# A spectral-mixing and attention stack with its stages woven together: one arena for all layers, work moved across the layer borders, and another share between two softmax paths

## The chip, the cores and the metric

The kernel runs on one core of one Trainium2 chip. The metric is the time of one execution on the device in microseconds (us). The core has five engines that run their own instruction streams in order: PE (matrix multiply; PEld are its weight loads), DVE (vector), ACT (scalar, activation functions), POOL and SP (here it only starts DMAs). Matmul results land in PSUM, which has 8 banks of 128 x 512 float32 in this program's tiling; everything else lives in SBUF.

## The reference, cut to what matters

```
x = A_x                                  # 1 x 2048 x 512, bfloat16
for _ in range(2):
    X = rfft2(layernorm(x)) * (w_r + 1j * w_i)
    x = x + irfft2(X)                                    # layer A, spectral
    n = layernorm(x)
    q = (n @ wq).reshape(32 heads, 2048, 16);  k = n @ wk;  v = n @ wv     # one k, v for all heads
    o = softmax(q k^T / 4) v                             # per head
    x = x + o.reshape(2048, 512) @ wo                    # layer B, attention
```

## The kernel before, in words

The 2048 rows of x lie in SBUF as `x_sb[128, r, t, 512]` with r and t from 0 to 3. Four rows r of one t belong together: the layer norm of a group t (`LayerNorm`, L87) takes statistics of its four slices as each is finished (`add`, L93: `bn_stats`, `bn_aggr` on DVE), then two small operations on POOL for 1/sqrt(var + eps) (L109, L110) and four scalings on DVE (L112) into `xn_sb`.

**Layer A** (`spectral_layer`, L149) works in three stages. Stage 1 goes over t: DVE makes sums and differences over r (L158 to L161), PE transposes them (L168), 16 matmuls against a Fourier table follow (L177), and ACT and DVE write the result to `Y`. Stage 2 goes over four groups j2: 48 matmuls of Y against the table `TAB` (L197 to L201), ACT copies the sums out (L203), and DVE multiplies them with the weights and combines them into `V` (L208 to L222). Stage 3 goes over t: 16 matmuls on V (L246), a copy by ACT and sums by DVE into `AT` (L251 to L253), and for each r five matmuls, one of them adding x (L256, L260); ACT writes x back (L262) and the layer norm's `add` follows. `TAB` is loaded with two of its six slots; POOL makes the negated slots and the repeated ones (L80 to L83).

**Layer B** (`attention_layer`, L270) begins when layer A is over. For four chunks qc of 512 rows, PE transposes xn (L129), and multiplies with the k weights twice, once for each of two zero-padded copies `wka` (L305); then come the four q projections of the first chunk (L289) and the v projection of all rows (L318). Only then does the loop start.

**The loop** (`AttnLoop`, L333) is written out by hand, and its engines keep this order (`manual_schedule`). It goes over 4 blocks qb of 512 query rows, 8 steps s of four heads each, here called stripes, so a layer has 32 stripes. Of the 16 chunks kc of 128 keys, 11 take the ACT path: two score matmuls into a double PSUM tile `sa`, one exponential on ACT over both into `e` (L463), and two steps later two matmuls with v into `acc`. The 5 chunks of `D_KC` take the DVE path: one score matmul into `sd`, DVE turns it into an int16 whose bits are a coarse power of two (`t0`, L467), two shifted copies by DVE (`tj`, L425) and one by POOL (L431) serve as further terms, and four matmuls with four scaled copies of v add them up. A stripe is 22 steps (`do_step`, L444), each with one ACT-path pair; in 20 of them there is a DVE-path unit as well. The two without are steps 10 and 21 of the stripe. They also carry the pieces: q projections of the next qb (L296, in s = 3 and 4), and the output projections of the last qb (`project`, L406, in s = 1 and 2), which add to x and, in the first attention layer, run the layer norm (L414, L100, L101, L112). `sa` and `sd` have two buffers each.

When a stripe's sums are complete, about eight steps into the next stripe, ACT copies `acc` to `den` (L374); SP moves the 4 rows of sums out (`dq`), DVE takes reciprocals six steps later (L381), SP sends them through DRAM and spreads them over the partitions (`rd`, `rb`), and ten steps later DVE normalises (`on_new` L397 for even s, `odd` L400 for odd s, which four DMAs then place into `on`). After the last step the loop runs on without new scores until all is drained (L510).

Both layers open and close their own SBUF and PSUM pools, and `full_kernel` (L516) runs A, B, A, B.

## Time and profile before

| | us |
|---|---|
| median of 5 runs (lowest, highest) | 1721.61 (1720.59, 1726.83) |
| the profiled execution, as timed | 1722.28 |
| its span, first to last instruction | 1720.5 |
| first attention loop, first exponential to last copy of sums | 709.18 |
| second attention loop, the same | 689.18 |

In the rows of the profile, times are us unless marked ns. A row of a group gives line, engine, operation, output and input tiles, count, then busy time, mean ns of one, idle time of the engine just ahead of it and what ended that. A row of a timeline gives start, length, engine, line, operation, and in brackets the idle time ahead and who released it. A row of the windows view gives, for a stretch of the span, its length, busy time and count of each engine, the TensorE clock granted (1.00 is full), and DMA. Busy times of overlapping instructions of one engine are not counted twice in sums over a stretch, but the mean length of one instruction includes the overlap with its neighbour.

### The profile page before, as it was taken

What the parts mean: (1) busy time and instruction counts of PE and PEld (TensorE: products, weight loads), DVE (VectorE), ACT (ScalarE), POOL (GpSimd) and SP (SyncE); (2) the same over time, 40 slices, a digit from 0 to 9 for tenths busy, and PEclk for the clock granted to TensorE, in tenths of its full rate; (3) what the DMA queues carried; (4) which work ended last, traced back from release to release, by engine and by line L of the source; (5) the groups of instructions that cost most, each with busy time, mean ns of one, the idle gap of its engine ahead of it and who ended that gap; (6) DMA issues with size and microseconds to landing.
All of it is one profiled execution on the core that took longest, in us unless ns stands there. A gap on an engine that the chain in (4) does not pass through costs nothing.

```text
span 1720.5 us, 34822 instructions
## 1 busy us (share of the span) xinstructions
PE 1535.9 (89%) x13536; PEld 484.5 (28%) x13536; DVE 1477.0 (86%) x2534; ACT 1427.0 (83%) x1607; POOL 720.8 (42%) x704
## 2 busy tenths in 40 slices
PE   0987999998999899989959799999999999999995
PEld 0543222222222222222225332222222222222221
DVE  3675999999999999999966769999999999999995
ACT  0434999998999899989923369999999999999993
POOL 6000444544444444444510115454545454545443
PEclk9998999999999999999989989999999999999997
DMA  6000000000000000000000000000000000000000
GB/s 175 1 1 1 8 16 16 16 16 16 16 16 16 11 15 17 15 15 16 16 15 1 1 1 15 16 16 16 28 16 16 16 28 16 16 16 28 16 16 29
DMA packets 39541, 31.78 MB, mean 18 GB/s; under 512 B 20800, under 2 KB 30160, under 8 KB 39248
## 3 DMA queue, kind: packets, MB, share of 16 engines
q1 hardware_dynamic: 38416, 27.31, 5.4%
q8 instruction: 106, 1.74, 0.4%
q0 software_dynamic: 960, 2.25, 0.4%
q14 instruction: 59, 0.48, 0.1%
HBM read 24.30 MB, written 2.62 MB: 16 GB/s over the span
## 4 chain that ended last, share of the span: by engine, by line
PE 55%; DVE 23%; ACT 12%; issue 4%; DMA 2%; POOL 2%; SPq 0%; ACTq 0%; DVEq 0%; POOLq 0%
PE acc_new L365 25%; PE sd L352 15%; ACT e L463 10%; DVE t L467 9%; PE sa L352 5%; DVE tj L425 3%; DVE on_new L397 2%; PE ps L412 2%; DVE odd L400 2%; PE ps L289 2%; DVE stats L100 2%; PE ps L197 2%; PE ps L177 1%; ACT den L374 1%; DVE xn_sb L112 1%
## 5 line engine op out<-in xcount | busy, mean ns | idle before, releaser
L463 ACT ACTIVATE e<-sa 128x1024 bf16<-128x1024 f32 x1408 | 1320.7, 1100 | 54.7 <-PE sa L352 51.8
L431 POOL TENSOR_SCALAR t<-tj 128x1024 int16<-128x1024 int16 x640 | 671.6, 1049 | 761.9 <-DVE tj L425 544.7
L467 DVE TENSOR_SCALAR t<-sd 128x512 int16<-128x512 f32 x1280 | 829.8, 678 | 66.6 <-PE sd L352 61.9
L352 PE MATMUL sa<-QT,KT 32*128 32x512 bf16 x2816 | 551.5, 384 | 12.3 <-ACT e L463 11.9
L365 PE MATMUL acc_new<-e,V 128*32 128x512 bf16 x2816 | 557.0, 392 | 1.0 <-ACT e L463 1.0
L352 PE MATMUL sd<-QT,KT 32*128 32x512 bf16 x1280 | 493.6, 386 | 59.9 <-DVE t L467 59.0
L425 DVE TENSOR_SCALAR tj<-t 128x2048 int16<-128x2048 int16 x640 | 438.0, 685 | 0.0
L365 PE MATMUL acc_new<-t,V 128*32 128x512 bf16 x2560 | 388.2, 387 | 1.0 <-POOL t L431 1.0
L365 PE MATMUL acc_new<-tj,V 128*32 128x512 bf16 x2560 | 386.9, 386 | 2.4 <-DVE tj L425 2.4
L352 PEld LDWEIGHTS <-KT 32*128 32x128 bf16 x4096 | 197.3, 91 | 675.6 <-issue 674.8
L365 PEld LDWEIGHTS <-V 128*32 128x32 bf16 x7936 | 159.0, 93 | 330.8 <-issue 330.3
L109 POOL TENSOR_TENSOR rstd<-mv,eps 128x4 f32<-128x4 f32 x16 | 3.7, 233 | 202.5 <-DVE mv L101 202.4
L170 ACT COPY xT<-ps 128x1024 bf16<-128x1024 bf16 x8 | 8.1, 1012 | 69.4 <-PE ps L168 69.4
L412 PE MATMUL ps<-wo_sb,on_new 128*128 128x512 bf16 x128 | 36.6, 419 | 25.7 <-DMA on_new<-odd 25.7
L100 DVE BATCH_NORM_STATS2 stats<-x_sb 128x6 f32<-128x512 bf16 x64 | 42.4, 678 | 12.4 <-ACT x_sb L262 8.3
L112 DVE TENSOR_SCALAR xn_sb<-x_sb,mv,rstd 128x512 bf16<-128x512 bf16 x64 | 22.0, 409 | 35.8 <-POOL rstd L110 35.8
L400 DVE TENSOR_TENSOR odd<-den,rb 128x512 bf16<-128x512 f32 x32 | 38.8, 1212 | 13.1 <-DMA rb<-rd 13.1
L203 ACT CAST Xs<-ps 128x512 bf16<-128x512 f32 x32 | 18.8, 586 | 36.8 <-PE ps L201 36.8
L197 PE MATMUL ps<-Y,tab_TAB 128*128 128x512 bf16 x128 | 48.5, 379 | 0.0
L168 PE MATMUL ps<-tab_ident,ec 128*128 128x128 bf16 x64 | 5.7, 241 | 46.5 <-DVE ec L159 43.8
L374 ACT COPY den<-acc_new 128x512 f32<-128x512 f32 x64 | 39.1, 611 | 8.1 <-PE acc_new L365 8.1
L414 DVE TENSOR_TENSOR x_sb<-ps,x_sb 128x512 bf16<-128x512 f32 x32 | 22.1, 690 | 24.5 <-PE ps L412 24.3
(81 smaller groups left out, 712.0 us busy)
## 6 DMA issues: line engine op xcount, KB each, us to landing
rb<-rd SPq DMA_DIRECT2D x64, 256.0 KB
x_sb<-in_A_x_dram SPq DMA_DIRECT2D x4, 512.0 KB
on_new<-odd SPq DMA_DIRECT2D x128, 16.0 KB
tab_TAB<-const_TAB SPq DMA_DIRECT2D x1, 1024.0 KB
wr_sb<-in_A_w_r_dram SPq DMA_DIRECT2D x4, 256.0 KB
wi_sb<-in_A_w_i_dram SPq DMA_DIRECT2D x4, 256.0 KB
dq<-den SPq DMA_DIRECT2D x64, 8.0 KB
rd<-dq SPq DMA_DIRECT2D x64, 8.0 KB
```

The source lines that it names most:

```text
L100: nc.vector.bn_stats(stats, self.x_sb[:, r, t, :])
L112: nc.vector.tensor_scalar(out=self.xn_sb[:, r, t, :], in0=self.x_sb[:, r, t, :], scalar1=mv[:, r, 0:1], scalar2=rstd[:, r:r + 1], op0=ALU. ...
L197: nc.tensor.matmul(ps, lhsT=TAB[:, t, j2, (COS + n) % 4, :], rhs=yt, start=(t == 0), stop=False, skip_group_check=True)
L352: self.nc.tensor.matmul(out, lhsT=self.KT[32 * i:32 * i + 32, half, kc * P:(kc + 1) * P], rhs=self.QT[32 * i:32 * i + 32, g, qb * 512:(qb ...
L365: self.nc.tensor.matmul(self.acc[key][32 * i:32 * i + 32, :], lhsT=self.V4[:, kc, j, :], rhs=e, start=first, stop=False, skip_group_check= ...
L374: nc.scalar.copy(out=den, in_=self.acc.pop(key))
L400: nc.vector.tensor_tensor(out=odd, in0=den, in1=rb, op=ALU.mult)
L412: nc.tensor.matmul(ps, lhsT=on[:, g, qt * P:(qt + 1) * P], rhs=self.wo_sb[:, g, :], start=(g == 0), stop=(g == 3))
L425: nc.vector.tensor_scalar(out=tj, in0=cyc["t0"], scalar1=float(SH[j]), scalar2=None, op0=ALU.add)
L431: nc.gpsimd.tensor_scalar(out=cyc["t1"][:, h, :], in0=tj[:, h, :], scalar1=1.0, scalar2=float(SH[1] - SH[j]), op0=ALU.mult, op1=ALU.add)
L463: nc.scalar.activation(out=e, in_=sa, func=ACT.Exp, bias=EXP_LN, scale=SCALE)
L467: nc.vector.tensor_scalar(out=self.dcyc[c]["t0"][:, k, :], in0=sd, scalar1=Y_MUL, scalar2=Y_ADD, op0=ALU.mult, op1=ALU.add)
```

## The change

The change rewrites how the layers are put together; what each engine computes for a layer is nearly the same.

- One SBUF arena and one PSUM arena serve the whole program (`Arena`, `make_arenas`). Tiles of layer A use the places of loop tiles (`ec` those of `t1`, `xTA` those of `t2`, `xc`, `dd`, `gh` those of `e`). PSUM is 2 double tiles "two", 2 tiles "one", 2 tiles "b", in banks as many as before. `den`, `rb` and `odd` have one buffer instead of two.
- At the start the first quarter of x is loaded first, then two small tables, then the other quarters, then the rest, all on SP. The layer norm and stage 1 of group t directly follow each other. The negated slots of TAB are made by ACT, the repeated ones by POOL, in the program's order after stage 1.
- The preparation of attention is cut by t (`prepare`): transposes, one k projection instead of two, whose two masked copies ACT and DVE write with `MASK`, and the v projection of that t. Each follows stage 3 of its t.
- ACT copies of stage 1 and 2 cover two banks where they covered one.
- In the loop, the normalisation is queued eight steps after the reciprocal and done just ahead of the next shift (`before_shift`). Pieces keep a distance of more than four steps. In the first attention layer, stripes s = 1 and 2 of qb = 1 to 3 have four DVE-path chunks and 24 steps, of which every third has no DVE-path unit. The last stripe of each loop has four DVE-path chunks, all in its first 16 steps. The four scalings of a layer norm are spread over four steps.
- What is left after the loop (`drain`) is outside the hand-written order, and so is stage 1 of the second layer A that follows.

```diff
+    nc.sync.dma_start(out=c.x_sb[:, :, 0, :], in_=x_v[:, :, 0, :])
+    table("ident")
+    table("PH")
+    for t in range(1, T):
+        nc.sync.dma_start(out=c.x_sb[:, :, t, :], in_=x_v[:, :, t, :])
...
+def expand_tab(nc, c):
     for u in range(4):
-        nc.gpsimd.tensor_scalar(out=tab[:, u, :, 2:4, :], in0=tab[:, u, :, 0:2, :], scalar1=-1.0, scalar2=None,
-                                op0=ALU.mult)
-        nc.gpsimd.tensor_copy(out=tab[:, u, :, 4:6, :], in_=tab[:, u, :, 0:2, :])
+        nc.scalar.mul(out=c.TAB[:, :, u, 2:4, :], in_=c.TAB[:, :, u, 0:2, :], mul=-1.0)
+        nc.gpsimd.tensor_copy(out=c.TAB[:, :, u, 4:6, :], in_=c.TAB[:, :, u, 0:2, :])
...
+    def prepare(self, t):
...
+        for cc in range(NC):
+            nc.tensor.matmul(pk, lhsT=c.wk[:, cc, :], rhs=xTq[:, cc, cols], start=(cc == 0), stop=(cc == NC - 1))
+        nc.scalar.activation(out=c.KT[:, 0, cols], in_=pk, func=ACT.Copy, scale=c.MASK[:, 0:1])
+        nc.vector.tensor_scalar(out=c.KT[:, 1, cols], in0=pk, scalar1=c.MASK[:, 1:2], scalar2=None, op0=ALU.mult)
...
+    def plan(self, qb, s):
+        if (qb, s) == (NQB - 1, 7):
+            return (1, 4, 7, 10), [a < 16 for a in range(24)]
+        if qb > 0 and s in (1, 2) and self.wide:
+            return (2, 5, 9, 12), [a % 3 != 2 for a in range(24)]
+        return (1, 4, 7, 10, 13), [a % 11 != 10 for a in range(22)]
...
-        self.at(10, lambda: self.normalize(key, den, rb))
+        self.at(8, lambda: self.before_shift.append(lambda: self.normalize(key, den, rb)))
...
     def shift(self, c, j):
         nc = self.nc
+        for fn in self.before_shift:
+            fn()
+        self.before_shift = []
...
-        if (d_unit is None or d_unit[0] is None) and self.pieces:
+        if u is None and self.pieces and self.step - self.last_piece > 4:
+            self.last_piece = self.step
             self.pieces.pop(0)()
...
+    for t in range(T):
+        for r in range(R):
+            ln_done(r, t)
+        spec.stage1(t)
+    expand_tab(nc, c)
+    for pair in range(n_pairs):
+        last = pair + 1 == n_pairs
+        spec.stage2()
+        at = Attention(nc, c, sb, ps, ln)
+        for t in range(T):
+            spec.final(t, ln_done)
+            if t == T - 1:
+                for g in range(4):
+                    at.qproj(0, g, g % 2 == 0)
+            at.prepare(t)
...
+        loop = AttnLoop(nc, c, at, work, dram, store if last else ln_loop, ln)
+        loop.wide = not last
+        with tc.manual_schedule(engines=LOOP_ENGINES):
+            loop.run()
+        loop.drain()
+        if not last:
+            spec = Spectral(nc, c, sb, ps, ln)
+            for t in range(T):
+                spec.stage1(t)
```

Three places show what this does to the order on an engine. On POOL at the start of the program, before, `rstd` is the layer norm's factor and `tab_TAB` the table:

```order
L109 TENSOR_TENSOR rstd<-mv,eps 128x4
L81 TENSOR_SCALAR tab_TAB<-tab_TAB 128x4x256
L83 COPY tab_TAB<-tab_TAB 128x4x256
L81 TENSOR_SCALAR tab_TAB<-tab_TAB 128x4x256
L83 COPY tab_TAB<-tab_TAB 128x4x256
L81 TENSOR_SCALAR tab_TAB<-tab_TAB 128x4x256
L83 COPY tab_TAB<-tab_TAB 128x4x256
L81 TENSOR_SCALAR tab_TAB<-tab_TAB 128x4x256
L83 COPY tab_TAB<-tab_TAB 128x4x256
L110 TENSOR_TENSOR rstd<-rstd,mhalf 128x4
```

The same place on POOL now:

```order
L169 TENSOR_TENSOR rstd<-mv,eps 128x4
L170 TENSOR_TENSOR rstd<-rstd,mhalf 128x4
L169 TENSOR_TENSOR rstd<-mv,eps 128x4
L170 TENSOR_TENSOR rstd<-rstd,mhalf 128x4
L144 COPY TAB<-TAB 128x4x256 x4
L169 TENSOR_TENSOR rstd<-mv,eps 128x4
```

The table's work stood between the two operations of the first layer norm; now the first two layer norms stand ahead of four copies, and the negations are gone from this engine.

On DVE at the end of the first attention loop, before, from the last shift; `odd` is the last normalisation, `x_sb` the output projection, `ec` and `xc` the inputs of stage 1:

```order
L425 TENSOR_SCALAR tj<-t_12485 128x2048
L381 RECIPROCAL dq<-dq 128x16
L400 TENSOR_TENSOR odd<-den,rb 128x512
L414 TENSOR_TENSOR x_sb<-ps,x_sb 128x512
L100 BN_STATS stats<-x_sb 128x6
L101 BN_AGGR mv<-stats 128x2
L414 TENSOR_TENSOR x_sb<-ps,x_sb 128x512
L100 BN_STATS stats<-x_sb 128x6
L101 BN_AGGR mv<-stats 128x2
L414 TENSOR_TENSOR x_sb<-ps,x_sb 128x512
L158 TENSOR_TENSOR ec<-xn_sb 128x1024
```

The same place on DVE now, from the third group's first sums:

```order
L200 TENSOR_TENSOR ec<-xn 128x1024
L201 TENSOR_TENSOR ec<-xn 128x1024
L418 RECIPROCAL dq<-dq 128x16
L202 TENSOR_TENSOR xc<-ec 128x512
L203 TENSOR_TENSOR xc<-ec 128x512
L225 TENSOR_TENSOR Y<-two,dd 128x256
L226 TENSOR_TENSOR Y<-two,dd 128x256
L227 TENSOR_TENSOR Y<-two,dd 128x256
L228 TENSOR_TENSOR Y<-two,dd 128x256
L213 COPY xTA<-one 128x1024
L434 TENSOR_TENSOR odd<-den,rb 128x512
```

Stage 1 of the groups whose layer norm is done stands around the last reciprocal and ahead of the last normalisation; before, it began after three of the four output projections.

On DVE in the loop, at the first normalisation (`on_new` before, `ON` now), in the second and third step of a stripe; `t` from `sd` or `b` is a score conversion, `t` or `tj` from `t` a shift. Before:

```order
L467 TENSOR_SCALAR t_1923<-sd 128x512 x2
L425 TENSOR_SCALAR tj<-t_1852 128x2048
L467 TENSOR_SCALAR t_1923<-sd 128x512
L397 TENSOR_TENSOR on_new<-den,rb 128x512
L467 TENSOR_SCALAR t_1923<-sd 128x512
```

Now:

```order
L492 TENSOR_SCALAR t_1872<-b 128x512 x2
L431 TENSOR_TENSOR ON<-den,rb 128x512
L459 TENSOR_SCALAR t_1897<-t_1801 128x2048
L492 TENSOR_SCALAR t_1872<-b 128x512 x2
```

The normalisation stands one conversion earlier, and the shift that stood ahead of it now stands behind it, so that both lie between the second and the third conversion of the stripe.

650 lines of the change are left out of this document (315 added, 335 removed), and 5 rows, old and new, of the table sb.

## The prediction

> **What bounds the kernel now.** I read the span stage by stage in the windows view, cut at the places where one stage hands over to the next. Its columns are the stretch, its length, the busy time of PE, PEld, DVE, ACT and POOL, the clock granted to TensorE, and DMA.
>
> ```profile
> 0.00:43.83 43.83, 0.00 (x0) 0.00 (x1) 17.64 (x53) 1.28 (x1) 29.93 (x32) 1.00 0.63 172
> 43.83:65.69 21.86, 20.84 (x128) 11.07 (x129) 14.02 (x33) 10.50 (x15) 0.00 (x0) 1.00 0.00 1
> 65.69:100.97 35.28, 32.44 (x213) 20.66 (x212) 26.25 (x51) 10.58 (x19) 0.00 (x0) 1.00 0.00 0
> 100.97:162.28 61.31, 49.28 (x306) 23.51 (x306) 36.24 (x81) 20.53 (x35) 4.83 (x8) 0.92 0.00 1
> 162.28:871.46 709.18, 663.93 (x6108) 185.82 (x6106) 654.08 (x1085) 671.61 (x735) 339.47 (x326) 0.99 0.05 15
> 871.46:914.40 42.94, 25.59 (x145) 12.71 (x145) 23.25 (x54) 11.09 (x16) 1.21 (x2) 0.80 0.03 8
> 914.40:949.50 35.10, 32.26 (x212) 20.58 (x211) 26.08 (x51) 10.60 (x19) 0.00 (x0) 1.00 0.01 1
> 949.50:1009.02 59.52, 47.59 (x306) 23.19 (x306) 36.23 (x81) 20.53 (x35) 4.83 (x8) 0.94 0.00 1
> 1009.02:1698.20 689.18, 658.20 (x6108) 185.11 (x6106) 639.51 (x1049) 669.74 (x736) 339.37 (x326) 1.00 0.06 18
> 1698.20:1720.50 22.30, 5.77 (x16) 1.80 (x15) 3.71 (x6) 0.57 (x1) 1.13 (x2) 0.58 0.12 39
> ```
>
> These ten add up to the span. The two attention loops are 1398 of 1720 us and full: ACT is busy for 95 and 97% of them. The other 322 us are not full: nothing runs on PE for 43.83 us at the start, and 100.97 to 162.28 has 12 us in which PE idles. So I look for gains outside the loops, and inside only where a loop waits.
>
> Next, what paces a loop. From the timeline of ACT and the chain of waits in the second loop:
>
> ```profile
> 1125.03 0.60 ACT L374 COPY den<-acc_new 128x512 f32<-128x512 f32 x1
> 1125.49 16.65 ACT L463 ACTIVATE e<-sa 128x1024 bf16<-128x1024 f32 x18
> ```
>
> ```profile
> 1139.87 1.17 DVE on_new L397
> 1160.97 1.17 DVE odd L400
> ```
>
> Eighteen exponentials without a gap take 16.65 us; less the length of one (1.1), one follows the other every (16.65 - 1.1) / 17 = 0.915 us. The copy of sums delays them by 0.46. A stripe at ACT's pace is then 22 x 0.915 + 0.46 = 20.6 us. Measured, from one normalisation to the next, it is 21.1. So ACT is the bound, and 0.5 us of each stripe is a wait.
>
> **The start.** The timeline of the first 60 us:
>
> ```profile
> 4.28 1.29 DVE L100 BATCH_NORM_STATS2 stats<-x_sb 128x6 f32<-128x512 bf16 x2 [3.38 <-DMA x_sb<-in_A_x_dram]
> 34.35 1.05 POOL L110 TENSOR_TENSOR rstd<-rstd,mhalf 128x4 f32<-128x4 f32 x1
> 35.44 1.38 DVE L112 TENSOR_SCALAR xn_sb<-x_sb,mv,rstd 128x512 bf16<-128x512 bf16 x4 [20.32 <-POOL rstd L110]
> 43.83 1.04 PE L168 MATMUL ps<-tab_ident,ec 128*128 128x128 bf16 x8 [43.83 <-DVE ec L159]
> 45.71 5.57 PE L177 MATMUL ps<-tab_PH,xT 128*128 128x512 bf16 x16
> 52.51 3.63 PE L177 MATMUL ps<-tab_PH,xT 128*128 128x512 bf16 x16 [0.34 <-DVE xT L172]
> ```
>
> POOL works on the table until the factor of the first layer norm runs at 34.35, and DVE idles 20.32 us for it. The change takes this out (the order of POOL above), and what is late next is DVE: layer norm and stage 1 are 17.64 + 14.02 = 31.7 us of its work, from 4.28 that is 36.0 without a wait. To it come the second quarter of x, now behind two tables, at most the 3.4 us that the first took; one factor from POOL for the last group, 1.3 with its small first operation; and the last 16 matmuls, 3.63 to 5.57. That makes 44.3 to 46.2; since the negations, now on ACT, wait for the table ahead of the first copies, I take the upper end: stage 2 starts at 46 instead of 65.69. **Gain 19.7**, bounds 14.5 (all matmuls slow) and 23 (x there in time).
>
> The first 16 matmuls after idleness took 5.57 us, later ones 3.63. The Trainium skill, "TensorE: Matmul & The Clock Gate", section "What's actually happening", says that the array runs at half its clock after about 3.4 us of idleness and needs as much sustained work to get it back; the rows agree. By that rule PE, which would now idle 3 to 4 us between groups, could stay at half clock through stage 1: the last matmuls would take 7.3 and stage 2 begin slow, an estimate of 51 instead of 46.
>
> **Stage 2 to the loop, twice.** Stage 2 keeps its work; a copy of two banks for one adds 0.4 at its end. Behind it PE has 49.28 us of work in 61.31. One group says what goes:
>
> ```profile
> L305 PE MATMUL ps<-xT,wka 128*128 128x512 bf16 x64 | 18.6, 442 | 13.4 <-DVE xT L135 13.4
> ```
>
> Half of these k projections vanish: 18.6 / 4 = 4.65 us per layer, which leaves 44.6 us of PE work. The 12 us of idleness come from waits that the work of another t now covers: the preparation of t - 1 stands between the matmuls of t. What stays is the last group: its layer norm (about 3 us, covered by the q projections, 16 matmuls like the 3.63 above), then copy, k projection and copy, some 2.2, and the first `AT` chain of stage 3, about 2. With 5 of idleness it is 49.6: gain 11.7, and 11.6 in the second layer; less 0.4 each. **Gain 22.5**; bounds 9.3 (only the projections go) and 32 (no idleness left).
>
> **The layer norm in the first loop.** The first loop is 709.18 - 689.18 = 20.0 us longer than the second. The first does the layer norm (14.6 us more of DVE, in s = 1 and 2 of three query blocks); all else is the same. There the change takes a fifth of DVE's units to ACT. Groups of the page and of the view of groups give the load, conversions and shifts first, then the addition to x and the statistics:
>
> ```profile
> L467 DVE TENSOR_SCALAR t<-sd 128x512 int16<-128x512 f32 x1280 | 829.8, 678 | 66.6 <-PE sd L352 61.9
> L425 DVE TENSOR_SCALAR tj<-t 128x2048 int16<-128x2048 int16 x640 | 438.0, 685 | 0.0
> L414 DVE TENSOR_TENSOR x_sb<-ps,x_sb 128x512 bf16<-128x512 f32 x32 | 22.1, 690 | 24.5 <-PE ps L412 24.3
> L100 DVE BATCH_NORM_STATS2 stats<-x_sb 128x6 f32<-128x512 bf16 x64 | 42.4, 678 | 12.4 <-ACT x_sb L262 8.3 <-DMA x_sb<-in_A_x_dram 3.6
> ```
>
> Such a stripe has 24 exponentials, 24 x 0.915 + 0.46 = 22.4 us. DVE has 16 x 0.65 + 8 x 0.68 and 1.5 for reciprocal and normalisation (rows below), 17.3. In s = 1 three output projections end on it, 3 x (0.69 + 0.68 + 0.2) = 4.7 by the last two rows, with their small aggregates: 22.0. In s = 2 come the fourth and the four scalings, 1.6 + 1.4: 20.3. Both stay below 22.4. So the 20.0 would be hidden; six such stripes cost 12 x 0.915 = 11.0 and save their waits, 6 x 0.5. **Gain 20.0 - 8.0 = 12**, bounds 2 (half of it hidden) and 13. Pieces and the second loop's stripes stay.
>
> **The normalisation's place, 58 ordinary stripes.** The wait of 0.5 us per stripe is made here; DVE (from the reciprocal that the normalisation needs) and PE in one stripe:
>
> ```profile
> 1130.93 0.25 DVE L381 RECIPROCAL dq<-dq 128x16 f32<-128x16 f32 x1
> ...
> 1137.98 0.69 DVE L467 TENSOR_SCALAR t<-sd 128x512 int16<-128x512 f32 x1 [0.44 <-PE sd L352]
> 1138.58 0.69 DVE L425 TENSOR_SCALAR tj<-t 128x2048 int16<-128x2048 int16 x1
> 1139.18 0.69 DVE L467 TENSOR_SCALAR t<-sd 128x512 int16<-128x512 f32 x1
> 1139.78 1.25 DVE L397 TENSOR_TENSOR on_new<-den,rb 128x512 bf16<-128x512 f32 x1
> 1140.96 0.68 DVE L467 TENSOR_SCALAR t<-sd 128x512 int16<-128x512 f32 x1
> ```
>
> ```profile
> 1140.31 0.38 PE L352 MATMUL sd<-QT,KT 32*128 32x512 bf16 x1
> 1141.69 0.37 PE L352 MATMUL sd<-QT,KT 32*128 32x512 bf16 x1 [0.40 <-DVE t L467]
> 1142.89 0.37 PE L352 MATMUL sd<-QT,KT 32*128 32x512 bf16 x1 [0.27 <-DVE t L467]
> ```
>
> A score matmul needs the conversion of two units back to be over. The normalisation makes the conversion of 1140.96 late, and PE waits 0.40 and then 0.27. In the new order normalisation and shift stand together behind the conversion of 1137.98: the next one starts at 1138.58 + 1.18 + 0.60 = 1140.36, ends at 1141.05, and the matmul of 1140.31 goes at 1141.1. One wait of 0.79 stands for two of 0.67 together. I take 0.05 us more per stripe, **a loss of 3**, bounds 7 lost and 2 won.
>
> **The ends of the loops and what follows.** From the timelines of ACT and DVE and from the chain of waits, at the end of the first loop, and one group of stage 1:
>
> ```profile
> 855.33 12.07 ACT L463 ACTIVATE e<-sa 128x1024 bf16<-128x1024 f32 x13
> 871.46 0.59 ACT L374 COPY den<-acc_new 128x512 f32<-128x512 f32 x1 [4.07 <-PE acc_new L365]
> ```
>
> ```profile
> 880.80 0.69 DVE L400 TENSOR_TENSOR odd<-den,rb 128x512 bf16<-128x512 f32 x1 [6.62 <-DMA rb<-rd]
> ```
>
> ```profile
> 875.65 5.03 DMA rb<-rd
> 885.27 5.00 PE ps L412 x13
> ```
>
> ```profile
> L159 DVE TENSOR_TENSOR ec<-xn_sb 128x1024 bf16<-128x1024 bf16 x8 | 5.5, 682 | 0.0
> ```
>
> The last DVE-path terms keep the sums open for 4.07 us after the last exponential. Now these end in step 16 of 24: two more exponentials (1.8), then some 0.6 to the copy. **Gain 1.6 per loop, 3.2**, bounds 0 and 4.
>
> From the copy at 871.46 to the projections at 885.27 is a chain of four DMAs, 13.8 us, that stays. Stage 1 of three groups now fills it. Behind it come the last matmuls of the projections (0.5), four additions and statistics (4 x 1.57 = 6.3), factor and scaling (1.3 + 1.4), sums (2 x 0.68 and two of half the size, 2.1), transposes and copy (1.9, from 43.83 to 45.71 above) and 16 matmuls (3.63): 31.0 instead of 42.94; 0.5 off for a clock that stood at 0.80 here. **Gain 11.5**, bounds 7 and 14. At the very end the same chain stays, with part of the projections done early: **gain 1**, bounds 0 and 2.
>
> **Rivals.** (1) *Half clock.* PE's work is cut into more and shorter pieces outside the loops. If the clock of 0.80 above held from stage 3 to the loop (0.92 and 0.94 now), 44.6 us of work would become 51.3 there and 42.9 become 50.4: 14 of the gain gone, with 5 at the start (its lower bound) and 6 at the join of the layers (the 16 matmuls twice as long, and the begin of stage 2). Gain 42, 1680 us. For it: the two sets of 16 matmuls above. Against: in stage 3 PE would idle less than now. This is what the Trainium skill's rule ("TensorE: Matmul & The Clock Gate", "What's actually happening") would do here. Chance 0.07.
> (2) *Slower than before.* The normalisation now comes 1.2 us earlier, and DVE waits there for `rb` with a shift and all later conversions behind it, and PE's scores and ACT behind these. From the reciprocal's end to `rb` DVE idles 6.62 us at the end of the loop (row above); in a stripe the new place, at 1138.58, leaves 7.4 behind the reciprocal of 1130.93. It decides from 0.8 us of lateness; each us beyond is 58 us. To eat the whole gain `rb` must land 2 us later than at the end of the loop; 3 us later makes 1780 us. Nothing here shows such a landing. Chance 0.03.
> (3) *The wide stripes only cost.* They are paid (8 us) and the layer norm's waits stay: 20 less gain, 1675 us. For it: DVE's load in one of them comes within a few us of 22.4. Chance 0.10.
> (4) *The shared places undo the overlap.* The order is as written, but a tile waits for its place in the arena, and preparation and stage 1 run after what they should cover: 13 and 11.5 less, 1679 us. Chance 0.06.
> (5) *The wait at the normalisation disappears*, since stripes of one kind now keep another rhythm: 58 x 0.5 + 3 more gain, 1622 us. Against it is the step worked out above. Chance 0.06.
>
> **How the numbers follow.** 19.7 + 22.5 + 12 - 3 + 3.2 + 11.5 + 1 = 66.9. The profiled execution took 1722.28 us, so 1655.4; it lies 0.67 above the median, hence 1654.7, rounded to 1655. This case has chance 0.68 and its own range of 1637 to 1673 by the bounds, which do not all fall on one side. With (1), (3) and (4) the range that holds 8 of 10 is 1634 to 1682. A measurement of this kernel tells about 0.3% (5 us) from no change. Only (2) and failures that I do not see end at or above the time before: faster 0.95, same 0.01, slower 0.04.
>
> **What would show it.** The first transposes before 20 us and stage 2 at 46; the first exponential some 50 us behind the end of V's sums; loops of about 697 and 689 us; stage 2 of the second layer A 30 to 32 us behind the copy of the last sums. A stripe of 21.1 us in the second loop would show the normalisation's step right; 20.6, or anything above 21.4, wrong. First and second loop still 20 us apart would refute the wide stripes, and idleness of DVE at the normalisation released by the DMA of `rb` would be rival (2).

## The result, and the profile after

The changed kernel takes 1638.18 us in the median of 8 runs (1631.86 to 1642.11), the kernel before, run beside it, 1722.82 us. The ratio is 0.9504, with a 95% interval of 0.9490 to 0.9518: 84.6 us less, where 67 had been forecast. The profiled execution took 1637.96 us with a span of 1636.2.

The windows view of the changed kernel, cut at its own hand-overs, answers to the table that the prediction opens with (stretch, length, busy time of PE, PEld, DVE, ACT and POOL, granted clock, DMA share, GB/s):

```profile
0.00:45.38 45.38, 24.59 (x131) 12.26 (x131) 33.82 (x84) 15.12 (x18) 12.31 (x22) 0.92 0.63 166
45.38:80.90 35.52, 31.62 (x207) 20.30 (x208) 25.71 (x48) 8.62 (x10) 0.00 (x0) 0.97 0.00 0
80.90:131.57 50.67, 43.60 (x291) 21.16 (x290) 35.94 (x78) 21.90 (x35) 8.65 (x19) 0.96 0.00 1
131.57:819.92 688.35, 670.10 (x6031) 190.28 (x6031) 621.07 (x1047) 677.28 (x750) 324.76 (x314) 0.99 0.05 15
819.92:852.11 32.19, 24.18 (x141) 11.97 (x139) 20.42 (x49) 10.30 (x13) 1.20 (x2) 0.89 0.04 11
852.11:887.20 35.09, 31.19 (x208) 20.20 (x208) 25.25 (x47) 8.75 (x9) 0.00 (x0) 1.00 0.00 1
887.20:939.19 51.99, 44.51 (x291) 21.50 (x290) 36.49 (x81) 21.91 (x34) 8.64 (x19) 0.93 0.00 1
939.19:1612.92 673.73, 659.80 (x6103) 184.62 (x6102) 618.15 (x1041) 666.16 (x737) 337.24 (x326) 0.99 0.06 18
1612.92:1636.20 23.28, 4.79 (x11) 1.27 (x10) 3.62 (x6) 0.58 (x1) 1.13 (x2) 0.68 0.11 37
```

Set against the table of before, stage by stage, in us:

| stage | before | after | gain | forecast |
|---|---|---|---|---|
| start to stage 2 | 65.69 | 45.38 | 20.3 | 19.7 |
| stage 2 to the first exponential, first layer | 96.59 | 86.19 | 10.4 | 11.3 |
| the same, second layer | 94.62 | 87.08 | 7.5 | 11.2 |
| first loop | 709.18 | 688.35 | 20.8 | } 12.2 for |
| second loop | 689.18 | 673.73 | 15.5 | } both loops |
| last sums to stage 2 | 42.94 | 32.19 | 10.8 | 11.5 |
| last sums to the end | 22.30 | 23.28 | -1.0 | 1.0 |
| sum | 1720.5 | 1636.2 | 84.3 | 66.9 |

Outside the loops the terms stand, a little short behind stage 2. The surplus is in the loops, 36.3 instead of 12.2. The second loop shows it plainly, since the forecast had nothing there but its end (1.6). DVE's timeline at two neighbouring normalisations of that loop, then POOL's and PE's at 1069:

```profile
1067.83 0.68 DVE L431 TENSOR_TENSOR ON<-den,rb 128x512 bf16<-128x512 f32 x1
1068.43 0.69 DVE L459 TENSOR_SCALAR t<-t 128x2048 int16<-128x2048 int16 x1
1069.03 1.28 DVE L492 TENSOR_SCALAR t<-b 128x512 int16<-128x512 f32 x2
...
1109.14 0.68 DVE L431 TENSOR_TENSOR ON<-den,rb 128x512 bf16<-128x512 f32 x1
...
1129.80 0.68 DVE L434 TENSOR_TENSOR odd<-den,rb 128x512 bf16<-128x512 f32 x1
```

```profile
1065.85 1.04 POOL L464 TENSOR_SCALAR t<-t 128x1024 int16<-128x1024 int16 x1 [0.66 <-DVE t L459]
1069.30 1.04 POOL L464 TENSOR_SCALAR t<-t 128x1024 int16<-128x1024 int16 x1 [2.41 <-DVE t L459]
```

```profile
1069.77 0.37 PE L389 MATMUL b<-QT,KT 32*128 32x512 bf16 x1 [0.15 <-DVE t L492]
```

The stripe from 1109.14 to 1129.80 takes 20.66 us, where the forecast had kept 21.1 and named 20.6 as the value that would refute its step on the normalisation. PE waits 0.15 us there instead of 0.40 and 0.27. And the multiply itself has become shorter. Its two lines in the view of groups, before (L397, L400) and after (L431, L434; the mean of one in ns stands behind the busy time):

```profile
L397 DVE TENSOR_TENSOR on_new<-den,rb 128x512 bf16<-128x512 f32 x32 | 39.6, 1237 | 0.8 <-ACT e L463 0.4 <-DMA rb<-rd 0.3
L400 DVE TENSOR_TENSOR odd<-den,rb 128x512 bf16<-128x512 f32 x32 | 38.8, 1212 | 13.1 <-DMA rb<-rd 13.1
```

```profile
L434 DVE TENSOR_TENSOR odd<-den,rb 128x512 bf16<-128x512 f32 x32 | 22.0, 689 | 10.5 <-DMA rb<-rd 9.7 <-ACT e L489 0.8
L431 DVE TENSOR_TENSOR ON<-den,rb 128x512 bf16<-128x512 f32 x32 | 21.8, 682 | 5.6 <-DMA rb<-rd 5.6
```

The same instruction on the same operands takes 1.24 us before and 0.68 after. POOL's timeline of before shows what stood beside it (DVE's rows of that place are in the prediction: the multiply ran from 1139.78 for 1.25 us):

```profile
1139.45 1.05 POOL L431 TENSOR_SCALAR t<-tj 128x1024 int16<-128x1024 int16 x1 [1.80 <-DVE tj L425]
```

POOL's half term of the shift had started 0.33 us earlier and was at work for another 0.72. In 62 of the 64 multiplies of before the pair lies like that; the other two are the last of each loop, where POOL is idle, with 0.69. So the theory: while POOL works, a DVE instruction that needs the same way into SBUF has to wait, and the multiply reads both operands from SBUF. The new place, ahead of the shift that sets POOL to work, takes it out of POOL's way. The rival: a multiply between two conversions makes PE wait, however long it takes, and the place alone has helped.

### The profile page after: what moved, and what is told of

It is laid out like the page before. It is cut to its first block, busy times and chain, and to the rows that moved or that the text cites. A ratio compares the mean times of both kernels' runs of the same rounds, so it can differ in the third digit from the quotient of the medians.

```text
span 1636.2 us, 34521 instructions
## 1 busy us (share of the span) xinstructions
PE 1534.4 (94%) x13408; PEld 483.6 (30%) x13408; DVE 1420.5 (87%) x2476; ACT 1430.6 (87%) x1602; POOL 693.9 (42%) x702
## 4 chain that ended last, share of the span: by engine, by line
PE 53%; ACT 27%; DVE 10%; issue 5%; DMA 3%; POOL 1%; SPq 0%; DVEq 0%; ACTq 0%; POOLq 0%
ACT e L489 25%; PE acc L402 23%; PE b L389 13%; PE sa L389 5%; DVE t L492 2%; PE one L305 2%; PE two L243 2%; PE b L445 2%; DVE t L459 2%; PE b L357 1%; ACT den L411 1%; DMA rb<-rd 1%; DVE xn L173 1%; PE two L219 1%; DVE stats L160 1%
## 5 line engine op out<-in xcount | busy, mean ns | idle before, releaser
L464 POOL TENSOR_SCALAR t<-t 128x1024 int16<-128x1024 int16 x624 | 653.2, 1047 | 683.9 <-DVE t L459 547.7
L492 DVE TENSOR_SCALAR t<-b 128x512 int16<-128x512 f32 x1248 | 807.4, 680 | 78.8 <-PE b L389 70.9
L402 PE MATMUL acc<-t,V 128*32 128x512 bf16 x4992 | 754.5, 386 | 0.0
L389 PE MATMUL sa<-QT,KT 32*128 32x512 bf16 x2848 | 558.3, 383 | 14.6 <-ACT e L489 14.4
L402 PE MATMUL acc<-e,V 128*32 128x512 bf16 x2848 | 563.3, 392 | 0.0
L389 PE MATMUL b<-QT,KT 32*128 32x512 bf16 x1248 | 480.7, 385 | 18.4 <-DVE t L492 13.2
L459 DVE TENSOR_SCALAR t<-t 128x2048 int16<-128x2048 int16 x624 | 427.4, 686 | 0.0
L445 PE MATMUL b<-wo_sb,ON 128*128 128x512 bf16 x128 | 35.5, 400 | 14.3 <-DMA ON<-odd 13.9
L243 PE MATMUL two<-Y,TAB 128*128 128x512 bf16 x128 | 48.5, 379 | 0.1
L411 ACT COPY den<-acc 128x512 f32<-128x512 f32 x64 | 43.7, 683 | 1.3 <-PE acc L402 1.3
L219 PE MATMUL two<-tab_PH,xTA 128*128 128x512 bf16 x128 | 35.0, 433 | 4.0 <-DVE xTA L213 4.0
```

Of the source, the lines that this page charges most:

```text
L219: nc.tensor.matmul(pm[:, q, :], lhsT=xT[:, pair, q, cc, :], rhs=c.PH[:, cc, :], start=(cc == 0), stop=(cc == NC - 1))
L243: nc.tensor.matmul(pm, lhsT=TAB[:, t, j2, (COS + n) % 4, :], rhs=yt, start=(t == 0), stop=False, skip_group_check=True)
L389: self.nc.tensor.matmul(out, lhsT=self.c.KT[32 * i:32 * i + 32, half, kc * P:(kc + 1) * P], rhs=self.A.QT[32 * i:32 * i + 32, g, qb * 512: ...
L402: self.nc.tensor.matmul(self.acc[key][32 * i:32 * i + 32, :], lhsT=self.c.V4[:, kc, j, :], rhs=e, start=first, stop=False, skip_group_chec ...
L411: nc.scalar.copy(out=den, in_=self.acc.pop(key))
L445: nc.tensor.matmul(po, lhsT=self.on[qb, g][:, r * P:(r + 1) * P], rhs=self.c.wo[:, g, :], start=(g == 0), stop=(g == 3))
```

## Experiments

**The multiply put back, behind the shift and the next conversion.**

```diff
         for fn in self.before_shift:
-            fn()
+            self.at(1, fn)
```

> The changed kernel with one thing put back: the normalisation's multiply stands behind the shift and the conversion that follows it, so that it starts while POOL works on its half term, as in the kernel before. Theory (POOL holds the multiply up): the multiply, which reads two operands from SBUF, takes about 1.25 us again instead of 0.68, and an ordinary stripe 21.1 us instead of 20.65; with some 58 such stripes the kernel takes 26 to 28 us longer, about 1665. Rival (place alone): a multiply that stands between two conversions makes PE wait wherever POOL is; also about 1665, but the multiply stays at 0.68. Second rival (the loops became shorter by other parts of the change): 1638 and stripes of 20.65.

1662.88 us, ratio 0.9641 (0.9616 to 0.9666), a stripe 21.10. DVE, then POOL, at one place:

```profile
1080.62 0.68 DVE L492 TENSOR_SCALAR t<-b 128x512 int16<-128x512 f32 x1
1081.22 1.25 DVE L431 TENSOR_TENSOR ON<-den,rb 128x512 bf16<-128x512 f32 x1
1082.39 0.68 DVE L492 TENSOR_SCALAR t<-b 128x512 int16<-128x512 f32 x1
```

```profile
1080.89 1.04 POOL L464 TENSOR_SCALAR t<-t 128x1024 int16<-128x1024 int16 x1 [1.80 <-DVE t L459]
```

In 54 of the 64 multiplies what stood before is there again: about 1.25 us and the overlap, and at the place shown PE's waits of 0.40 and 0.27. This one place is worth about 24 us (1662.88 against 1638.18, 0.9641 against 0.9504). Length and place return together, so the run alone doesn't separate the theories.

**The multiply directly behind the shift.** It is called between the shift on DVE and POOL's half term.

```diff
-        for fn in self.before_shift:
-            fn()
-        self.before_shift = []
+        fns, self.before_shift = self.before_shift, []
...
         cyc[f"t{j}"] = tj
+        for fn in fns:
+            fn()
         if j == 2:
```

> The changed kernel with the multiply directly behind the shift, no conversion between. It then starts some 0.6 us after the shift's start, POOL's half term some 0.87 after it. Theory (whichever of the two starts first keeps the other waiting): the multiply starts first and takes 0.68, POOL's half term takes longer instead (1.05 becomes 1.3 to 1.5); a stripe stays at 20.65 and the time within 3 us of 1638. Rival (place alone): behind the shift is behind the shift; the next conversion is late and a stripe takes 21.1, about 1665. Rival (any overlap with POOL slows the multiply): 1.2 us for the multiply and about 1665.

1640.43 us, 0.9513 (0.9488 to 0.9539), a stripe 20.65. DVE, then POOL:

```profile
1064.96 0.68 DVE L459 TENSOR_SCALAR t<-t 128x2048 int16<-128x2048 int16 x1
1065.56 0.69 DVE L431 TENSOR_TENSOR ON<-den,rb 128x512 bf16<-128x512 f32 x1
```

```profile
1065.83 1.32 POOL L466 TENSOR_SCALAR t<-t 128x1024 int16<-128x1024 int16 x1 [1.81 <-DVE t L459]
```

Now the multiply starts 0.27 us before POOL, keeps its 0.69, and POOL's term takes 1.32 instead of 1.04. Whichever of the two starts first keeps the other waiting. The same trace has the other order too: at 199.67 and 284.77 the multiply comes late, POOL has started less than 0.1 us ahead of it, and it takes 1.55 and 1.50. In these places and in the runs around, the one that waits is longer by nearly what was left of the other: 0.57 of 0.71 in the first run, 0.28 of 0.42 here, 0.87 of 1.01 at 199.67, always about 0.14 less.

**POOL's term held until the multiply is over**, in the order of the first run:

```diff
+                y = fn()
+                probe = self.work.tile([P, 1], BF, tag="probe", bufs=2)
+                nc.gpsimd.tensor_copy(out=probe, in_=y[:, 0:1])
...
+        if fns:
+            self.at(1, part)
```

> The changed kernel with DVE's order as in the run with the multiply behind the shift and the next conversion, but POOL's half term in these steps is held until the multiply is over, by a copy of one column of the product on POOL ahead of it. Theory (POOL holds the multiply up): the multiply takes 0.68 in the same place on DVE, a stripe 20.65, the time 1638 to 1643. Rival (place alone): 21.1 a stripe and about 1665, as without the hold.

1661.13 us, 0.9640 (0.9619 to 0.9661), a stripe 21.12: the number of the rival. But DVE and POOL show another cause than place:

```profile
1078.21 0.68 DVE L431 TENSOR_TENSOR ON<-den,rb 128x512 bf16<-128x512 f32 x1
1078.81 0.68 DVE L504 TENSOR_SCALAR t<-b 128x512 int16<-128x512 f32 x1
1079.41 1.28 DVE L460 TENSOR_SCALAR t<-t 128x2048 int16<-128x2048 int16 x1
```

```profile
1079.10 1.04 POOL L471 TENSOR_SCALAR t<-t 128x1024 int16<-128x1024 int16 x1
```

The multiply has its 0.68, as the theory said. The held term now runs into the next shift, which takes 1.28 instead of 0.68, and PE waits 0.70 behind that. I had not seen that the shift can be held up too. The conversion between them, which reads PSUM, keeps 0.68 with POOL beside it. It had started ahead of POOL, but the same holds behind it: in the changed kernel the second of the two conversions from 1069.03 starts when POOL has been at work for 0.3 us, and takes 0.68 too.

**POOL's term left out in these steps**, again in the order of the first run:

```diff
+        if leave:
+            cyc[h.start] = cyc[h.start + 1] = tj
+            return
         nc.gpsimd.tensor_scalar(out=cyc["t1"][:, h, :], in0=tj[:, h, :], scalar1=1.0, scalar2=float(SH[1] - SH[j]),
```

> The kernel of the run with the multiply behind the shift and the next conversion (1662.9), without POOL's half term in the steps that have a multiply: the half term is left out there, and the sums take the shifted term itself in its place, so a tenth of one of the four terms has slightly other weights. Nothing on POOL then stands against the multiply or the shift behind it. Theory (POOL holds up the multiply, and, in the run that held POOL's term back, the shift of 128x2048 behind it, 1.28 instead of 0.68): multiply and shift both 0.68, PE's wait 0.15 as in the changed kernel, a stripe 20.65, the time about 1638. Rival (place alone: any multiply behind the shift costs 0.45 a stripe): 21.1 and about 1662.

1633.60 us, 0.9478 (0.9459 to 0.9496), a stripe 20.66. DVE's order is that of the first run, word for word, and nothing is slow:

```profile
1065.15 0.68 DVE L496 TENSOR_SCALAR t<-b 128x512 int16<-128x512 f32 x1
1065.75 0.68 DVE L431 TENSOR_TENSOR ON<-den,rb 128x512 bf16<-128x512 f32 x1
1066.35 0.69 DVE L496 TENSOR_SCALAR t<-b 128x512 int16<-128x512 f32 x1
1066.95 0.69 DVE L459 TENSOR_SCALAR t<-t 128x2048 int16<-128x2048 int16 x1
```

In the same place and without POOL beside it the multiply costs nothing: the rival falls, and the theory is shown. The median lies 4.6 us below that of the changed kernel. In the traces 2.8 us of difference stand at the start of the second loop (first sums 28.15 us behind the first exponential instead of 30.94), which has to do with PE's clock, as the last runs below show.

**The kernel before, with the normalisation ahead of the shift and nothing else.**

```diff
-        self.at(10, lambda: self.normalize(key, den, rb))
+        self.at(8, lambda: self.before_shift.append(lambda: self.normalize(key, den, rb)))
...
+            if k in (1, 3):
+                for fn in self.before_shift:
+                    fn()
+                self.before_shift = []
             if k == 1 and c - 1 in self.dcyc:
...
```

> The kernel before with one part of the change alone: the normalisation stands ahead of the shift. Theory (POOL holds the multiply up): the multiply goes from 1.24 to 0.68 and ordinary stripes from 21.1 to 20.65: 60 x 0.45 = 27 us less, about 1695. Rival of the prediction's step (one wait of 0.79 stands for two of 0.67): about 1725. Rival (the loops became shorter by other parts of the change): 1722.

1696.33 us, 0.9843 (0.9826 to 0.9860): 26.6 us less than the kernel before, run beside it, multiplies of 0.68, stripes of 20.65. The loops take 698.50 and 674.56 us and are now 23.9 apart: the first one keeps its layer norm.

**No wide stripes.**

```diff
-        loop.wide = not last
+        loop.wide = False
```

> The changed kernel without the wide stripes: all stripes but the last have 22 steps. The first loop was 14.6 us longer than the second with them (688.4 and 673.7), 20.0 before the change. Theory (the wide stripes hide most of the layer norm and cost 12 x 0.915 = 11): without them the first loop is 18 to 20 us longer than the second, so the kernel 4 to 6 us longer, about 1643. Rival (they only cost; the free place of the normalisation leaves DVE room enough for the layer norm): the difference of the loops falls to 4 or less and the time by 11, 1627.

1636.87 us, 0.9500 (0.9468 to 0.9532): no difference that this measurement shows. The loops take 688.64 and 674.00 us, as with wide stripes. Theory and rival named 4 to 6 us more and 11 less, and both are wrong: in this kernel the six wide stripes cost about what they save. What then hides the layer norm?

**No wide stripes, and the four scalings together.**

```diff
-                ln.apply(t, loop.at if t < NQB - 1 else None)
+                ln.apply(t)
...
-        loop.wide = not last
+        loop.wide = False
```

> The changed kernel without the wide stripes (1636.9, its first loop 14.6 us longer than the second) and with the four scalings of the layer norm in the loop issued together, directly behind the statistics, as before the change, and not one by one from the fourth step on. Theory (what shortened the first loop's layer norm is this spreading: together they make DVE wait for POOL's factor, with all conversions behind them): the first loop becomes 20 to 24 us longer than the second, as in the kernel before with the multiply ahead of the shift (698.5 and 674.6), and the time 6 to 9 us longer, about 1644. Rival (the spreading does nothing, and the gain came from the piece's place or the shared arena): 1637.

1647.76 us, 0.9556 (0.9543 to 0.9570): about 10 more than without wide stripes alone. DVE and ACT at one layer norm:

```profile
370.21 0.18 DVE L161 BATCH_NORM_AGGREGATE mv<-stats 128x2 f32<-128x6 f32 x1
371.83 1.38 DVE L173 TENSOR_SCALAR xn<-x_sb,mv,rstd 128x512 bf16<-128x512 bf16 x4 [1.43 <-POOL rstd L170]
```

```profile
374.37 2.06 ACT L489 ACTIVATE e<-sa 128x1024 bf16<-128x1024 f32 x2 [3.25 <-PE sa L389]
```

DVE stands 1.43 us for POOL's factor with all conversions behind it, then does four scalings in a row; PE's scores wait, and ACT has nothing for 3.25 us. Spread one per step from the fourth step on, as the change does, the largest gap of ACT at this place in the run before is 0.50.

The kernel before shows the same at its first layer norm, on DVE and on ACT:

```profile
402.58 1.38 DVE L112 TENSOR_SCALAR xn_sb<-x_sb,mv,rstd 128x512 bf16<-128x512 bf16 x4 [1.41 <-POOL rstd L110]
```

```profile
405.31 1.02 ACT L463 ACTIVATE e<-sa 128x1024 bf16<-128x1024 f32 x1 [3.42 <-PE sa L352]
```

From 401.20 to 404.60 PE is busy there for 0.03 of 3.40 us, and for the next 3.41 us its granted clock is 0.50. The clock falls at all three layer norms of that loop, and at all three here; in the changed kernel and in the run without wide stripes it falls at none.

The size was not what was expected. The time is 10.9 us longer, not 6 to 9, and in the trace, the slowest of the six executions (1656.61), the loops are 31.0 apart, not 20 to 24. At six multiplies in the middle of this first loop DVE waits for the DMA of `rb`, 6.2 us together; the run without wide stripes has four such waits, 2.4 us. Differences of one or two us between the first loops of single traces therefore say little.

**The plan of the last stripe undone**, with the branch for it in `run`:

```diff
-        if (qb, s) == (NQB - 1, 7):
-            return (1, 4, 7, 10), [a < 16 for a in range(24)]
```

> The changed kernel with the plan of the last stripe undone: 22 steps, DVE units to the end. Theory (the last terms of DVE's path keep the sums open): the copy of the last sums comes about 4 us behind the last exponential instead of 0.65, the last stripe has two exponentials less; each loop 1.0 to 1.6 us longer, about 1641. Rival (the two more exponentials cost what the shorter end saves): 1638.

1641.18 us, 0.9508 (0.9492 to 0.9524); the ratio does not tell it from the changed kernel, the traces do: the copy of the last sums comes 5.20 and 4.23 us behind the last exponential instead of 0.65, and the loops take 690.08 and 675.49, 1.7 and 1.8 longer, a little more than expected.

**Preparation behind the last layer norm of the spectral layer.** The unit matrix for its transposes is a copy that depends on the last scaling. The four q projections move with it, from ahead of the last preparation to behind the first.

```diff
             spec.final(t, ln_done)
+        one = work.tile([P, 1], F32, tag="one", bufs=1)
+        nc.vector.tensor_scalar(out=one, in0=ln.xn[T - 1][:, R - 1, 0:1], scalar1=0.0, scalar2=1.0, op0=ALU.mult, op1=ALU.add)
+        at.ident = work.tile([P, P], BF, tag="ident2", bufs=1)
+        nc.vector.tensor_scalar(out=at.ident, in0=c.ident, scalar1=one[:, 0:1], scalar2=None, op0=ALU.mult)
+        for t in range(T):
+            at.prepare(t)
...
```

> The changed kernel with the preparation of the attention put behind the last layer norm of the spectral layer (its transposes read a copy of the unit matrix that is written only then), so that the work of one t no longer covers the waits of another. Theory (the gain between stage 2 and the loop comes from this cover, 7 us per layer, beside 4.65 from the halved k projections): 7 to 12 us longer per layer, 1652 to 1662. Rival (the halved projections are all of it): at most 3 us per layer, 1644 or less.

1668.03 us, 0.9666 (0.9648 to 0.9684). This is above the range expected. The first exponential comes 15.0 us later in the first layer, and in the second 11.1 later behind the last sums: with what goes along with it the cover is worth about the 12 us of idleness that the prediction had read from the profile. From stage 2 to the first exponential PE idles for 20.9 and 20.4 us instead of 11.0 and 11.4, and its clock is 0.92 and 0.91 instead of 0.96.

**Table work on POOL ahead of the first factor.**

```diff
+    expand_tab(nc, c)
+    nc.gpsimd.tensor_scalar(out=c.eps, in0=c.TAB[:, 3, 3, 5, 0:R], scalar1=0.0, scalar2=EPS, op0=ALU.mult, op1=ALU.add)
     spec = Spectral(nc, c, sb, ps, ln)
...
```

> The changed kernel with the table work as before: POOL negates and copies it ahead of the first factor of the layer norm (the small constant that the factor needs is written from the table's last part). Theory (the first factor waits for POOL's table): the table lands at about 15.3 us, POOL's work on it takes 15, the first scaling starts at about 31.5 instead of 11.5; stage 2 starts at 60 to 62 instead of 45.4: 15 to 17 us longer, 1654. Rival (the start is bound by the landing of x and of the table, and by DVE): at most 8 us longer, 1646 or less.

1653.35 us, 0.9572 (0.9544 to 0.9599). The time is 15.2 us longer, as expected; stage 2 starts at 59.6 instead of 45.4, a little ahead of the 60 to 62 expected.

**One wide stripe for two, and PE kept busy.** The groups of matmuls write a PSUM tile that nobody reads.

```diff
-        if qb > 0 and s in (1, 2) and self.wide:
+        if qb > 0 and s == 2 and self.wide:
...
+        if t == 1:
+            warm(nc, ps, spec.xT[:, 0, 1, 3, :], c.PH[:, 3, :], 8)
...
         loop.drain()
+        if last:
+            warm(nc, ps, c.ident, c.PH[:, 3, :], 54)
...
+                if t == 2:
+                    warm(nc, ps, spec.xT[:, 0, 1, 3, :], c.PH[:, 3, :], 16)
```

> The changed kernel with two edits in different places. First, wide stripes only at s = 2: by the theory that a wide stripe costs 2 x 0.915 and takes load from DVE where the scalings stand, the first loop becomes 8 to 12 us longer than the second instead of 14.6 (3 to 6 us gain); by the rival (with the multiply free, wide or not is the same) it stays at 14 to 15. Second, matmuls whose results nobody reads fill idle stretches of PE: 8 in the start, 16 in the join between the loops and 54 behind the last sums. By the theory that PE runs at half clock after such a stretch, the last 16 matmuls of the join take 3.6 instead of 5.3 and their transposes 1.2 instead of 2.1, the last ten matmuls of the kernel 2.2 to 3.5 instead of 4.5, and the start gets up to 2 shorter: 4 to 7 us gain. By its rival (those matmuls wait for DVE or a DMA anyway) at most 1. Together 1626 to 1632 by the theories, 1637 by the rivals.

1628.57 us, 0.9449 (0.9432 to 0.9467): the sum that the two theories gave, but not all by their parts. From the copy of the first sums to that of the last, the first loop takes 652.4 us (657.8 in the changed kernel), the second 642.9 (642.8): one wide stripe for two is worth about 5. Against none at all (659.3 us) it is 6.9, so that by these single traces the wide stripe s = 2 pays and s = 1 costs about as much. The loops as a whole are 13.4 apart, not 8 to 12, since the clock fell at the start of the first loop and not of the second. In the join, changed kernel and this run:

```profile
844.53 1.03 PE L209 MATMUL one<-tab_ident,ec 128*128 128x128 bf16 x8 [5.60 <-DVE ec L201]
845.35 1.06 PE L209 MATMUL one<-tab_ident,xc 128*128 128x128 bf16 x8
846.35 5.37 PE L219 MATMUL two<-tab_PH,xTA 128*128 128x512 bf16 x16
```

```profile
844.00 0.62 PE L209 MATMUL one<-tab_ident,ec 128*128 128x128 bf16 x8 [0.57 <-DVE ec L201]
844.45 0.61 PE L209 MATMUL one<-tab_ident,xc 128*128 128x128 bf16 x8
845.40 3.63 PE L219 MATMUL two<-tab_PH,xTA 128*128 128x512 bf16 x16 [0.34 <-DVE xTA L213]
```

After 5.60 us of idleness the same work takes 7 us, without it 5. At the very end the last ten matmuls take 2.5 us instead of 4.5, and the stretch behind the last sums 1.7 less. But the join as a whole is not shorter here, 32.3 us against 32.2: `rb` landed later (the last normalisation starts 10.9 us behind the last sums instead of 9.4). The start became 0.8 us longer. Another 2.8 us come from the start of the second loop, where the clock did not fall this time, and nothing in the edit was meant for that place.

**The clock held elsewhere too.** The start of the first loop in the changed kernel, in the windows view (the clock is the third number from the end):

```profile
126.30:129.70 3.40, 1.87 (x20) 1.15 (x19) 2.28 (x5) 1.01 (x1) 0.00 (x0) 1.00 0.02 5
129.70:133.10 3.40, 2.41 (x31) 1.23 (x28) 2.20 (x5) 2.22 (x3) 1.11 (x3) 1.00 0.00 0
133.10:143.40 10.30, 10.30 (x53) 1.88 (x51) 7.12 (x11) 8.62 (x10) 2.47 (x3) 0.50 0.00 0
```

PE never idles for 0.8 us at a stretch in the 3.4 us ahead of 133.10; it is busy for 2.41 of 3.40, with small matmuls, and then gets half its clock for the next 10.3 us. Its busy time alone does not tell when this happens: in the 3.4 us before, it was busy for 1.87 only, and no fall followed. There stood transposes and matmuls over all 128 rows, here mostly matmuls of 32 rows (scores) or with 16 columns (v); whether that is the difference was not tested. This run adds full-sized matmuls there, too:

```diff
+        if self.step < 10:
+            if self.step == 0:
+                self.idle = self.ps.tile("one", [P, 512], F32)
+            nc.tensor.matmul(self.idle, lhsT=self.c.ident, rhs=self.c.PH[:, 3, :], start=True, stop=True)
...
```

> The run with one wide stripe and filled idle stretches (1628.6), with more of PE's idle stretches filled by matmuls that nobody reads: 20 ahead of the first transposes, 8 more in the start, 10 in each wait for V, 4 beside the last q projections, and one in each of the first ten steps of a loop. In its trace the granted clock still fell to half for 3 to 14 us in each of these places, and the first sums of a loop were copied 31.97 us behind the first exponential where it fell, 28.15 where it didn't. Theory (these falls follow PE's light use just before, and cost what PE's work there doubles): no fall behind V and at the loops' starts, the first sums 28.1 to 29 us behind the first exponential in both loops, the clock of the whole above 0.99: 3 to 8 us less, 1621 to 1626. Rival (PE waits there for DVE or ACT anyway, and the added matmuls in the loop only delay the scores): 1628 to 1632.

1621.19 us, 0.9403 (0.9390 to 0.9416), the fastest of all, with a mean clock of 0.997 in the trace (0.981 in the changed kernel). ACT at the beginning of the second loop, changed kernel and this run:

```profile
939.19 5.75 ACT L489 ACTIVATE e<-sa 128x1024 bf16<-128x1024 f32 x6 [0.47 <-PE sa L389]
...
970.13 0.82 ACT L411 COPY den<-acc 128x512 f32<-128x512 f32 x1
```

```profile
923.17 8.65 ACT L489 ACTIVATE e<-sa 128x1024 bf16<-128x1024 f32 x9 [0.47 <-PE sa L389]
931.98 20.52 ACT L489 ACTIVATE e<-sa 128x1024 bf16<-128x1024 f32 x22 [0.16 <-PE sa L389]
952.13 0.85 ACT L411 COPY den<-acc 128x512 f32<-128x512 f32 x1
```

The first sums come 28.96 us behind the first exponential instead of 30.94, and stage 2 to the first exponential takes 83.8 us in both layers instead of 86.2 and 87.1. The join takes 29.8 us instead of 32.2. The start, filled as well, stays as it was (stage 2 at 45.1 instead of 45.4).

## Why the prediction was right, and where not

The forecast held, direction and range, with 17 us between the likeliest case and the time. That the range held is in part luck: the step on the normalisation was off by 27 us, more than the 21 between the likeliest case and the lower end of the range, and shortfalls behind stage 2, in the join and at the end gave some 7 back. By its own steps:

- **The start** (19.7 forecast, 20.3 measured): right. With POOL's table work put back ahead of the factors, stage 2 begins 14.2 us later.
- **Stage 2 to the loop** (22.5, 17.9): the mechanism is right, the idleness that stays was mis-sized. PE idles 7.1 and 7.5 us there instead of 5, and the clock, which the step left out, took some: in the last run, with the clock held, the two stretches gain 12.7 and 10.8 us against before, 23.5 together.
- **The layer norm in the first loop** (12 by the wide stripes): wrong in its cause. The step added up DVE's load and put its wait for POOL's factor at nothing, though that wait and the four scalings in a row leave ACT without work for 3.42 us in the kernel before, and the clock falls behind it. Without wide stripes the time is the same, and the spread scalings, which the step passed over, are worth about 10. The size came out as forecast only where the multiply stood in its old place: with it there the loops take 697.4 and 688.7 us, and 697 and 689 was what the forecast gave. That is a coincidence. With the multiply free, ordinary stripes become 0.45 us shorter, but three stripes with a layer norm together hardly (67.9 us with the multiply in its old place, 67.5 without), which puts the loops some 3 us further apart. They are 14.6 apart instead of 8.7; the rest lies in single stripes, one of which waits for `rb` (below).
- **The normalisation's place** (a loss of 3; measured, a gain of about 24): the step that failed. It read "the next one starts at 1138.58 + 1.18 + 0.60 = 1140.36" and took the 1.18 from a row in which POOL held the multiply up. With the 0.60 from one start to the next that the multiply needs alone, the same step gives 1139.78, an end of the conversion at 1140.47 and a wait of 0.16 for the matmul of 1140.31; 0.15 was measured. The prediction had quoted 1.25 and, at the end of the loop, 0.69 for the same operation on tiles of the same shape, and did not ask why. The Trainium skill has the rule ("SBUF — State Buffer", section "Who interferes with whom"): a DVE instruction with two inputs from SBUF contends with a GpSimd instruction that reads SBUF, and so does one in the fast modes that use both of DVE's ports; the shared pair is an exclusive lock, and the order of issue decides who waits. The runs agree for the multiply and POOL's term: 1.25 for 0.68, 1.32 for 1.04. The shift has one input, so by the page it would have to run in such a mode; that it handles 2048 columns in the 0.68 us in which a conversion handles 512 fits this, and behind POOL it takes 1.28.
- **Rival (5)**, "the wait at the normalisation disappears", had a chance of 0.06 and is what happened to the wait, though not for the reason given there (another rhythm). It priced this at 1622; the layer norm, which it took as hidden, and the shortfalls behind stage 2 and at the end kept the time above that.
- **The ends of the loops** (3.2, and 3.5 by the trace of the run without the plan) and **the join** (11.5, 10.8): right.
- **The very end** (a gain of 1, a loss of 1): the last ten matmuls take 4.5 us at a clock of about half; the 13 of before took 4.63.
- **Rival (1)**, half clock, is real, though before has it as well: filling the idle stretches and making one stripe wide for two took 17.0 us off the changed kernel, of which about 5 belong to the stripe.
- **Rival (2)**, the wait for `rb`, is seen once in the middle of a loop of the changed kernel:

```profile
735.92 0.69 DVE L431 TENSOR_TENSOR ON<-den,rb 128x512 bf16<-128x512 f32 x1 [1.30 <-DMA rb<-rd]
```

From one copy of sums to the next that stripe takes 22.0 us instead of 20.6. The kernel before and the run with the multiply put back have no such wait in mid-loop; runs with the multiply ahead of the shift have up to six, nearly all in the first loop. Why there was not examined. It is far from the lateness of 2 us in every stripe that this rival needed. Of rival (4) nothing is seen: the overlap is there.

## What to carry to other kernels

Before a duration is carried into a new order of instructions, ask what ran beside it: if the same instruction has two durations in one trace, the difference is a term of its own. Put a DVE instruction that reads two SBUF operands ahead of the instruction that sets GpSimd to work, as long as its operands are there by then, and spread what waits for GpSimd over later steps. And where a loop begins with little PE work, look at the granted clock: at the start of this loop ten matmuls into an unused PSUM tile cost 0.8 us (first sums at 28.96 instead of 28.15), the fall of the clock 1.2 to 4.1 us.

## What the runs showed of the hardware

The granted clock fell to half for about 3.4 us or a multiple of that, and not only after idleness: at the start of a loop 2.41 of 3.40 us of PE work with small matmuls was followed by such a fall, where 1.87 of 3.40 just before had not been. The Trainium skill ("TensorE: Matmul & The Clock Gate", section "What's actually happening") speaks of a free-running window of about 3.4 us, which agrees, and of an idle one ahead of a fall; here the one ahead of a fall was not idle. Whether the fall came differed between executions: the first sums of a loop stand 28.1 to 32.3 us behind its first exponential over the profiles of these runs. It may be a part of the 10 us by which the runs of the changed kernel differ; how much was not measured.
